# Sigmoid attention feeding a SiLU layer: a weight load in smaller pieces, another order of products in the output sets, and other stores at the end

## The chip, the cores and the metric

The kernel runs on one core of a Trainium2 chip. The metric is the time of one execution in microseconds (us) on the device; lower is better. TensorE (PE in the profile, PEld for its weight loads) multiplies matrices into PSUM, VectorE (DVE) and ScalarE (ACT) work on tiles, GpSimd (POOL) here issues all loads but the first, and SyncE (SP) issues the stores and the transposing DMAs.

## What is computed

Inputs are float32: q, k, v of shape (8, 12, 448, 64) and the weights w_in (768, 2048) and w_out (2048, 768).

```python
scores = (q @ k.transpose(0, 1, 3, 2)) / sqrt(64) - log(448)
attn = sigmoid(scores) @ v                      # (8, 12, 448, 64)
x = attn.transpose(0, 2, 1, 3).reshape(3584, 768)
h = x @ w_in
out = (h * sigmoid(h)) @ w_out                  # (3584, 768)
```

## The kernel before, in words

**Attention.** The work is cut into 24 groups g (a batch b and four of its heads). A group has seven chunks of keys. `scores` (L165) makes the 128x2x448 score tile of a chunk (64 keys, four heads) with four matmuls of 64 rows (L174), and ScalarE turns it into float16 with a sigmoid (L181). `values` (L191) multiplies the seven tiles by v (28 matmuls, L205) and scales the result into `xT`, the transposed input of the layer (L217, L221). The first six groups' q and k are transposed by TensorE (`pe_transpose`, L135), the rest by transposing DMAs.

**The layer.** The batches are taken in four pairs m. For the first pair `h_unit` (L234) makes one 128-column piece fc of h for one batch: six matmuls with w_in's columns fc*128 to fc*128+127 (L240), a sigmoid on ScalarE (L252) and a product on VectorE (L253). Pieces 0 to 7 need the first half of w_in's columns, pieces 8 to 15 the second half. After piece 8 and later ones of batch 0, VectorE also makes sums of w_in's blocks (`w_in_sums`, L272), the first of which reads all of the second half. For the later pairs `h_pair` (L300) uses a seven-product scheme in place of eight (in the manner of Strassen and Winograd). Its result lies in `gTr`.

**The output sets.** `out_set` (L442) multiplies two blocks of 128 rows by w_out with seven products of eight matmuls each (L463), also in the seven-product scheme. VectorE makes the sums S of the rows' blocks (`sg`, L478, L479, L484, L493), ScalarE copies the first product to `m1` (L481), and `plus` (L472) adds a product from PSUM to a block of the output tile `osb` (an eviction, L473). The output tiles are c11 and c12 (the two column halves of the first 128 rows) and c21 and c22 (of the second). `store` (L453) sends each tile in two halves of 64 rows (L455). There are 14 sets: three for each pair of batches, and one more after every second pair. The four that come first after a pair's h have a `tail`: their sums are made by then. The other ten make their own sums, at their start. In these, before the change, the order of the products is a1, a1 high, sg[2], sg[1], a2 high, sg[0], sg[3], with eight evictions. The very last set (`last`) computes c21 late and the last product in two halves of 192 columns.

**Order.** TensorE's order is written out by hand. `stretch` (L608) takes steps from the generator `all_moe` (L582) until its count of estimated nanoseconds is due, and between stretches `attend` (L746) puts in scores and values. Each `yield` is one matmul. The order on every engine is fixed when the program is built.

**Loads.** Loads go through POOL's queue, in program order, and convert to float16 on the way. `load` (L79) brings one group of q, k or v (224 KB as float16). `load_w_in(step, steps)` (L103) brings a range of w_in's columns with two DMAs, one for each half of its rows: at L642 and L644 a quarter of the columns each (384 KB a DMA), at L651 half of the columns (768 KB a DMA). `load_w_out` (L112) brings 768 KB. The calls stand in `after_transpose` (L640) and `after_values` (L648). Four buffers hold q and k, three hold v.

Of the kernel before, what the change touches and what calls it, by code (L numbers as in the profile page):

```python
# [17 lines left out]
def kernel(  # L18
# [9 lines left out]
    nc = tc.nc  # L28

    B, H, S, D = q.shape  # L30
    NT, DMODEL = out.shape
    DFF = moe_w_in.shape[1]
# [8 lines left out]
    NO2 = DMODEL // 2  # L41
    NQB = NQ * B
    NHC = NFC // 2
# [22 lines left out]
    def new_flat(name, g):  # L66
        flat[name, g] = (p3 if name == "v" else p4).tile(
            [P, 2, NCH, D], F16, tag=f"{name}f", name=f"{name}f"
        )

    def rows_in(name, g):
        b, iq = divmod(g, NQ)
        return (
            source[name][b]
            .rearrange("(j h) s d -> j h s d", j=2)[:, 2 * iq : 2 * iq + 2]
            .rearrange("j h (p c) d -> (h p) j (c d)", c=NCH)
        )

    def load(names, g, c0=0, c1=NCH):  # L79
        for name in names:  # L80
            if (name, g) not in flat:
                new_flat(name, g)
            nc.gpsimd.dma_start(  # L83
                flat[name, g][:, :, c0:c1].rearrange("p j c d -> p j (c d)"),
                rows_in(name, g)[:, :, c0 * D : c1 * D],
            )
# [13 lines left out]
    w_in_of = w_in_sb.rearrange("p (q h) f -> p h q f", h=2)  # L100
    w_out_sb = cpool.tile([P, NFC, DMODEL], F16, tag="w_out_sb", name="w_out_sb")

    def load_w_in(step, steps=1):  # L103
        cols = slice(step * DFF // 4, (step + steps) * DFF // 4)
        for j in range(2):
            rows = slice(j * DMODEL // 2, (j + 1) * DMODEL // 2)
            nc.gpsimd.dma_start(
                w_in_sb[j * D : (j + 1) * D, :, cols],
                moe_w_in[rows, cols].rearrange("(cc d) f -> d cc f", d=D),
            )  # L110

    def load_w_out(part):  # L112
        fcs = slice(part * NFC // 4, (part + 1) * NFC // 4)
        nc.gpsimd.dma_start(
            w_out_sb[:, fcs],
            moe_w_out[part * DFF // 4 : (part + 1) * DFF // 4].rearrange("(fc p) e -> p fc e", p=P),
        )
# [182 lines left out]
    def h_pair(m, tail):  # L300
# [112 lines left out]
    wq = [  # L413
        [w_out_sb[:, r * NHC : (r + 1) * NHC, c * NO2 : (c + 1) * NO2] for c in range(2)]
        for r in range(2)
    ]
    tw = {}
# [18 lines left out]
    def block(g):  # L436
        return gTr[:, :, g * P : (g + 1) * P]

    def row_blocks(m, g):
        return [rows_of[2 * m + u // NCH, u % NCH] for u in (2 * g, 2 * g + 1)]  # L440

    def out_set(a1, rows1, a2, rows2, scale, tail=(), last=False, halves=False):  # L442
        nonlocal hold
        lo, hi = slice(0, NHC), slice(NHC, NFC)
        osb = [p3.tile([P, DMODEL], F32, tag="osb", name="osb") for _ in range(2)]
        c11, c12 = (osb[0][:, nh * NO2 : (nh + 1) * NO2] for nh in range(2))
        c21, c22 = (osb[1][:, nh * NO2 : (nh + 1) * NO2] for nh in range(2))
        m1 = p3.tile([P, S], F32, tag="m1", name="m1")[:, :NO2]
        between, *sg = tail or [None]
        for i in range(len(sg) + 1, 4):  # L450
            sg.append(cpool.tile([P, NHC, P], F16, tag=f"S{i}", name=f"S{i}"))

        def store(rows, o, cols, engines):  # L453
            for at, (row, eng) in enumerate(zip(rows, engines)):
                eng.dma_start(row[:, cols], o[at * HP : (at + 1) * HP, cols])  # L455

        left, right, whole = slice(0, NO2), slice(NO2, DMODEL), slice(0, DMODEL)

        def product(a, w, between=None):
            po = ps_1.tile([P, 512], F32, tag="ps1", name="po")  # L460
            n = w.shape[2]
            for fc in range(NHC):
                nc.tensor.matmul(  # L463
                    po[:, :n], a[:, fc, :], w[:, fc, :], start=(fc == 0), stop=(fc == NHC - 1)
                )
                if fc < NHC - 1:
                    yield 163
                if between and fc == NHC // 2 - 1:
                    yield from between()
            return po[:, :n]  # L470

        def plus(o, po, x, sign=1.0):  # L472
            nc.vector.scalar_tensor_tensor(  # L473
                out=o, in0=po, scalar=sign * scale, in1=x, op0=ALU.mult, op1=ALU.add
            )

        if not tail:
            nc.vector.tensor_sub(sg[2], a1[:, lo], a2[:, lo])  # L478
            nc.vector.tensor_add(sg[0], a2[:, lo], a2[:, hi])  # L479
        po = yield from product(a1[:, lo], wq[0][0], between)  # L480
        nc.scalar.activation(m1, po, AF.Copy, scale=scale)  # L481
        sg.append(cpool.tile([P, NHC, P], F16, tag="S4", name="S4"))
        if not tail:
            nc.vector.tensor_sub(sg[1], sg[0], a1[:, lo])  # L484
        hold = False
        yield 163
        if tail:
            po = yield from product(sg[2], tw[3])
            plus(c22, po, m1)
            yield 163  # L490
        po = yield from product(a1[:, hi], wq[1][0])
        plus(c11, po, m1)
        nc.vector.tensor_sub(sg[3], a1[:, hi], sg[1])  # L493
        if last or halves:
            store(rows1, osb[0], left, (nc.sync, nc.sync))
        yield 163
        if not tail:
            po = yield from product(sg[2], tw[3])
            plus(c22, po, m1)
            yield 163  # L500
        po = yield from product(sg[1], tw[2])
        both = c21 if last else c22
        plus(both, po, c22)
        plus(c12, po, m1)
        yield 163

        def minus():
            po = yield from product(a2[:, hi], tw[4])
            plus(c21, po, both, -1.0)
            if not last:  # L510
                yield 163

        if not last:
            yield from minus()
        po = yield from product(sg[0], tw[1])
        plus(c22, po, both)
        plus(c12, po, c12)
        if last:
            yield 163
            yield from minus()  # L520
        store(rows2, osb[1], whole, (nc.sync, nc.scalar if last else nc.sync))
        yield 163
        for c0 in (0, NO2 // 2) if last else (0,):
            c1 = NO2 // 2 + c0 if last else NO2
            po = yield from product(sg[3], wq[1][1][:, :, c0:c1])
            plus(c12[:, c0:c1], po, c12[:, c0:c1])
            if last:
                store(rows1, osb[0], slice(NO2 + c0, NO2 + c1), (nc.sync, nc.scalar))
        if not last:
            store(rows1, osb[0], right if halves else whole, (nc.sync, nc.sync))  # L530
        yield 163

# [23 lines left out]
            if b * NFC + fc in rows_at:  # L556
                rows_of_quad(*rows_at[b * NFC + fc], act_copy)

    HALVES = 0

    def moe_set(m, g, tail=()):
        scale = ISX if m == 0 else 1.0
        step = out_set(
            block(g),
            row_blocks(m, g),
            block(g + 1),
            row_blocks(m, g + 1),
            scale,
            tail,
            halves=(m == B // 2 - 1 and g >= HALVES),  # L570
        )
        for i, ns in enumerate(step):
            if m % 2 == 0 and g == 2 and i % 8 == 4 and i < 32:
                fcs = slice(i // 8 * 4, i // 8 * 4 + 4)
                nc.vector.tensor_scalar_mul(kept[:, fcs], block(NCH - 1)[:, fcs], scale)
            if m == 0 and g == 2 and i in (36, 44, 52):
                next(in_sums)
            if m == 0 and g == 0 and i in (2, 8, 14, 20):
                next(sums)
            yield ns  # L580
# [59 lines left out]
    def after_transpose(g):  # L640
        if g == 0:
            load_w_in(0)  # L642
            load("kq", 4)
            load_w_in(1)  # L644
        elif g == 1:
            load("kq", 5)

    def after_values(g):  # L648
        if g == 0:
            load("v", 3)  # L650
            load_w_in(2, 2)  # L651
        elif g == 1:
            load("v", 4)
            load_w_out(0)
            load_w_out(2)
        elif g == 2:
            load("v", 5)
            load("kq", 6)
            load_w_out(1)
            load("kq", 7)  # L660
            load_w_out(3)
        elif 4 < g < NQB - 3:
            load("v", g + 3)
# [34 lines left out]
    def rounds(g, end):  # L698
        values(g, end)
        if end == NCH:  # L700
            after_values(g)
# [77 lines left out]
    n = 2 * NT_B  # L779
    for m in range(1, B // 2):  # L780
        stop = min(2 * (m + 1) * NT_B + 4, len(units))
        bursts = bursts_to(n, stop)
        n = stop
# [51 lines left out]
```

## Time and profile before

| | us |
|---|---|
| three runs | 364.54, 363.94, 367.28 |
| their median | 364.54 |
| the profiled execution | 367.21 |
| its span, from the first instruction's start to the last one's end | 365.1 |
| PE busy in it | 355.9 |
| DVE, ACT, POOL busy | 265.0, 249.7, 61.8 |

The profile is of one execution, the one of 367.21 us; 2.1 us of it lie outside the span. Lines are named L and a number. A row of the timeline gives the start, the busy time of a run of equal instructions and, in brackets, how long the engine had been idle before and what ended that. A landing is the moment when a DMA's completion is signalled. "POOL ... <- DMA x" in the list of waits means that POOL waited for the landing of x before it could issue.

### The profile page before, as it was taken

How to read it: one execution, taken by the hardware profiler on the slowest of the kernel's cores; microseconds unless marked ns; L12 is line 12 of the kernel's file. 1: busy time of each engine (PE TensorE's matmuls, PEld its weight loads, DVE VectorE, ACT ScalarE, POOL GpSimd, SP SyncE). 2: the span in 40 equal slices, each digit the busy share in tenths (PEclk: the TensorE clock that was granted, in tenths of full speed). 3: DMA queues.
4: the chain of work that ended last, by engine and by line, in shares of the span. 5: the costliest groups of instructions: out<-in, count | busy, mean ns of one | idle time of the engine just before them, and what ended most of it. 6: DMA issues, size and time to landing. Idle time of an engine off the chain costs nothing.

```text
span 365.1 us, 7677 instructions
## 1 busy us (share of the span) xinstructions
PE 355.9 (97%) x3029; PEld 182.9 (50%) x3029; DVE 265.0 (73%) x498; ACT 249.7 (68%) x363; POOL 61.8 (17%) x103
## 2 busy tenths in 40 slices
PE   8999799999999999999999999999999999999995
PEld 4544345444454555555445455555445455556663
DVE  3647479887879678787677667786777677778773
ACT  5998587697778767678777767758888766660000
POOL 8543210412505001100222201200100000000000
PEclk9999899999999999999999999999999999999999
DMA  8999999999899838405999752731965020003333
GB/s 136 196 205 210 208 206 170 135 195 139 139 202 175 147 95 114 59 0 96 172 165 216 148 113 50 105 49 24 154 95 133 19 69 0 3 0 87 88 87 85
DMA packets 63106, 42.78 MB, mean 117 GB/s; under 512 B 36064, under 2 KB 59232, under 8 KB 63072
## 3 DMA queue, kind: packets, MB, share of 16 engines
q0 software_dynamic: 24096, 22.58, 41.3%
q1 hardware_dynamic: 38592, 19.21, 26.9%
q10 hardware_dynamic: 384, 0.52, 0.4%
q8 instruction: 23, 0.38, 0.4%
q14 instruction: 11, 0.09, 0.1%
HBM read 45.61 MB, written 11.01 MB: 155 GB/s over the span
## 4 chain that ended last, share of the span: by engine, by line
PE 89%; DMA 9%; DVE 1%; issue 0%
PE po L463 36%; PE hy L316 11%; PE psc L174 10%; PE ph L240 8%; PE hz L316 7%; PE hx L316 7%; PE pav L205 7%; DMA w_in_sb<-in_moe_w_in_dram 5%; DMA kf<-in_k_dram 3%; DMA qs<-in_q_dram 1%; DVE qT L150 1%; PE ptrq L143 0%; PE pw L130 0%; PE ptrk L143 0%; DVE qf L633 0%
## 5 line engine op out<-in xcount | busy, mean ns | idle before, releaser
L181 ACT ACTIVATE attnT<-psc 128x896 f16<-128x896 f32 x168 | 144.9, 922 | 32.5 <-PE psc L174 29.9
L463 PEld LDWEIGHTS <-S 128*128 128x128 f16 x456 | 42.2, 98 | 35.5 <-issue 10.4
L174 PE MATMUL psc<-qT,kT 64*64 64x448 f16 x672 | 52.2, 361 | 1.0 <-DVE qT L150 0.7
L473 DVE SCALAR_TENSOR_TENSOR osb<-po,osb 128x384 f32<-128x384 f32 (+1 forms) x71 | 37.8, 549 | 15.9 <-PE po L463 15.0
L221 DVE TENSOR_SCALAR xT<-pav 128x448 f16<-128x448 f32 x44 | 25.6, 620 | 26.0 <-PE pav L205 26.0
L327 ACT ACTIVATE gTr<-u 128x448 f16<-128x448 f32 x48 | 27.6, 575 | 23.2 <-DVE u L340 19.1
L240 PE MATMUL ph<-xT,w_in_sb 128*128 128x448 f16 x192 | 40.5, 361 | 2.7 <-DMA w_in_sb<-in_moe_w_in_dram 2.6
L463 PE MATMUL po<-w_out_sb,S 128*128 128x384 f16 (+1 forms) x232 | 41.5, 321 | 0.0
L463 PE MATMUL po<-T,S 128*128 128x384 f16 x224 | 41.3, 327 | 0.0
L316 PEld LDWEIGHTS <-w_in_sb 128*128 128x128 f16 x288 | 28.2, 98 | 26.1
L463 PEld LDWEIGHTS <-gTr 128*128 128x128 f16 x304 | 28.3, 98 | 23.2 <-issue 5.8
L205 PE MATMUL pav<-attnT,vf 64*64 64x448 f16 x672 | 37.5, 349 | 0.0
L463 PE MATMUL po<-w_out_sb,gTr 128*128 128x384 f16 x192 | 35.7, 327 | 0.0
L316 PE MATMUL hy<-xs,w_in_sb 128*128 128x448 f16 x144 | 35.1, 353 | 0.0
L316 PE MATMUL hx<-xT,w_in_sb 128*128 128x448 f16 x144 | 34.6, 353 | 0.0
L316 PEld LDWEIGHTS <-W 128*128 128x128 f16 x216 | 21.1, 98 | 19.6
L174 PEld LDWEIGHTS <-kT 64*64 64x64 f16 x672 | 16.2, 104 | 28.8 <-issue 24.2
L83 POOL DMA_DIRECT2D vf<-in_v_dram x24 | 17.2, 718 | 71.6 <-PE psc L174 70.0
L240 PEld LDWEIGHTS <-w_in_sb 128*128 128x128 f16 x192 | 17.7, 99 | 23.0 <-issue 8.9
L473 DVE SCALAR_TENSOR_TENSOR osb<-po,m 128x384 f32<-128x384 f32 x42 | 23.0, 553 | 6.4 <-PE psc L174 1.7
L253 DVE TENSOR_TENSOR gTr<-ph,tsig 128x448 f16<-128x448 f32 x32 | 19.8, 623 | 9.1 <-ACT tsig L252 8.9
L205 PEld LDWEIGHTS <-vf 64*64 64x64 f16 x672 | 20.1, 107 | 11.5 <-issue 1.1
(76 smaller groups left out, 414.4 us busy)
## 6 DMA issues: line engine op xcount, KB each, us to landing
out_dram<-osb SPq DMA_DIRECT2D x47, 192.0 KB, 3.2
vf<-in_v_dram POOLq DMA_DIRECT2D x24, 224.0 KB, 7.8
kf<-in_k_dram POOLq DMA_DIRECT2D x23, 224.0 KB, 5.8
qf<-in_q_dram POOLq DMA_DIRECT2D x23, 224.0 KB, 6.8
w_out_sb<-in_moe_w_out_dram POOLq DMA_DIRECT2D x4, 768.0 KB, 18.4
w_in_sb<-in_moe_w_in_dram POOLq DMA_DIRECT2D x4, 384.0 KB, 11.4
w_in_sb<-in_moe_w_in_dram POOLq DMA_DIRECT2D x2, 768.0 KB, 15.1
out_dram<-osb SPq DMA_DIRECT2D x14, 96.0 KB, 2.2
```

Of the source, the lines that this page charges most:

```text
L83: nc.gpsimd.dma_start(flat[name, g][:, :, c0:c1].rearrange("p j c d -> p j (c d)"), rows_in(name, g)[:, :, c0 * D : c1 * D],)
L150: (copy[0] if copy else nc.vector.tensor_copy)(dst[:, c0 * P : c1 * P], ptr[:, : (c1 - c0) * P])
L174: nc.tensor.matmul(psc[own, j, :S], qkT["k", g][rows, ch, own], qkT["q", g][rows, :, own], start=True, stop=True,)
L181: nc.scalar.activation(attnT[g, ch], psc[:, :, :S], AF.Sigmoid, bias=NEG_LOG_S, scale=QKSCALE)
L205: nc.tensor.matmul(pav[half][j * D : (j + 1) * D, :S], flat["v", g][own, j, ch, :], at[own, j, :], start=(ch == 0), stop=(ch == NCH - 1),)
L221: nc.vector.tensor_scalar_mul(xT[b][:, half * NQ + iq, :], pav[half][:, :S], SX)
L240: nc.tensor.matmul(ph[:, :S], w_in_of[:, cc // NQ, cc % NQ, fc * P : (fc + 1) * P], xT[b][:, cc, :], start=(at == 0), stop=(at == NCC - 1),)
L253: nc.vector.tensor_mul(gTr[:, fc, (b % 2) * S : (b % 2) * S + S], ph[:, :S], tsig)
L316: nc.tensor.matmul(ps, a[:, c, i * P : (i + 1) * P], bs(c), start=(first and c == 0), stop=(c == HCC - 1), skip_group_check=True,)
L327: nc.scalar.activation(gTr[:, side * NHC + i, odd * S : (odd + 1) * S], src, AF.Silu, scale=ISX)
L463: nc.tensor.matmul(po[:, :n], a[:, fc, :], w[:, fc, :], start=(fc == 0), stop=(fc == NHC - 1))
L473: nc.vector.scalar_tensor_tensor(out=o, in0=po, scalar=sign * scale, in1=x, op0=ALU.mult, op1=ALU.add)
```

## The change

Three parts. First, the second half of w_in is loaded as two quarters (four DMAs of 384 KB) in place of one half (two of 768 KB), and among the loads before it group 4's q is moved behind w_in's second quarter. Second, in the ten sets without a tail, sg[1] is multiplied before sg[2], and c22 is started from c12, which already holds m1 plus sg[1]'s product; one eviction falls away, and sg[0] and sg[1] are now made at the set's start and sg[2] after the first product's copy. The four sets with a tail keep their products and evictions. Third, the very last set follows the same order as the others, computes c21 before sg[0]'s product, stores c21 and c22 as two column halves on the queues of SP and ACT, and makes and stores the last product's 384 columns in one piece.

```diff
-    def load_w_in(step, steps=1):
-        cols = slice(step * DFF // 4, (step + steps) * DFF // 4)
+    def load_w_in(step):
+        cols = slice(step * DFF // 4, (step + 1) * DFF // 4)
...
         if not tail:
-            nc.vector.tensor_sub(sg[2], a1[:, lo], a2[:, lo])
             nc.vector.tensor_add(sg[0], a2[:, lo], a2[:, hi])
+            nc.vector.tensor_sub(sg[1], sg[0], a1[:, lo])
         po = yield from product(a1[:, lo], wq[0][0], between)
         nc.scalar.activation(m1, po, AF.Copy, scale=scale)
+        if not tail:
+            nc.vector.tensor_sub(sg[2], a1[:, lo], a2[:, lo])
         sg.append(cpool.tile([P, NHC, P], F16, tag="S4", name="S4"))
-        if not tail:
-            nc.vector.tensor_sub(sg[1], sg[0], a1[:, lo])
...
+        po = yield from product(sg[1], tw[2])
+        if tail:
+            plus(c22, po, c22)
+        plus(c12, po, m1)
+        yield 163
         if not tail:
             po = yield from product(sg[2], tw[3])
-            plus(c22, po, m1)
+            plus(c22, po, c12)
             yield 163
-        po = yield from product(sg[1], tw[2])
-        both = c21 if last else c22
-        plus(both, po, c22)
-        plus(c12, po, m1)
+        po = yield from product(a2[:, hi], tw[4])
+        plus(c21, po, c22, -1.0)
+        if last:
+            store(rows2, osb[1], left, (nc.sync, nc.scalar))
         yield 163
-
-        def minus():
-            po = yield from product(a2[:, hi], tw[4])
-            plus(c21, po, both, -1.0)
-            if not last:
-                yield 163
-
-        if not last:
-            yield from minus()
         po = yield from product(sg[0], tw[1])
-        plus(c22, po, both)
+        plus(c22, po, c22)
         plus(c12, po, c12)
         if last:
-            yield 163
-            yield from minus()
-        store(rows2, osb[1], whole, (nc.sync, nc.scalar if last else nc.sync))
+            store(rows2, osb[1], right, (nc.sync, nc.scalar))
+        else:
+            store(rows2, osb[1], whole, (nc.sync, nc.sync))
         yield 163
-        for c0 in (0, NO2 // 2) if last else (0,):
-            c1 = NO2 // 2 + c0 if last else NO2
-            po = yield from product(sg[3], wq[1][1][:, :, c0:c1])
-            plus(c12[:, c0:c1], po, c12[:, c0:c1])
-            if last:
-                store(rows1, osb[0], slice(NO2 + c0, NO2 + c1), (nc.sync, nc.scalar))
-        if not last:
+        po = yield from product(sg[3], wq[1][1])
+        plus(c12, po, c12)
+        if last:
+            store(rows1, osb[0], right, (nc.sync, nc.scalar))
+        else:
             store(rows1, osb[0], right if halves else whole, (nc.sync, nc.sync))
         yield 163
...
             load_w_in(0)
-            load("kq", 4)
+            load("k", 4)
             load_w_in(1)
+            load("q", 4)
...
             load("v", 3)
-            load_w_in(2, 2)
+            load_w_in(2)
+            load_w_in(3)
```

The name HALVES, which was 0 and chose nothing, is dropped; `product` always takes 384 columns.

More of the change, by code (lines that the diff above doesn't have):

```diff
@@ L460, in product @@
             po = ps_1.tile([P, 512], F32, tag="ps1", name="po")
-            n = w.shape[2]
             for fc in range(NHC):
                 nc.tensor.matmul(
-                    po[:, :n], a[:, fc, :], w[:, fc, :], start=(fc == 0), stop=(fc == NHC - 1)
+                    po[:, :NO2], a[:, fc, :], w[:, fc, :], start=(fc == 0), stop=(fc == NHC - 1)
                 )
@@ L469, in product @@
                     yield from between()
-            return po[:, :n]
+            return po[:, :NO2]
         def plus(o, po, x, sign=1.0):
@@ L557, in moe_h @@
                 rows_of_quad(*rows_at[b * NFC + fc], act_copy)
-    HALVES = 0
     def moe_set(m, g, tail=()):
@@ L569, in moe_set @@
             tail,
-            halves=(m == B // 2 - 1 and g >= HALVES),
+            halves=(m == B // 2 - 1),
         )
```

## The prediction

> **What bounds the kernel now.** I read the page first, then TensorE's list of waits, then the timeline and the chain around its only long wait, then POOL's loads one by one, and last the end.
>
> ```profile
> PE 355.9 (97%) x3029; PEld 182.9 (50%) x3029; DVE 265.0 (73%) x498; ACT 249.7 (68%) x363; POOL 61.8 (17%) x103
> ```
> ```profile
> PE ph L240 <- DMA w_in_sb<-in_moe_w_in_dram: 2.6, 1, 2.6
> ...
> PE psc L174 <- DVE qT L150: 0.7, 2, 0.4
> ```
>
> TensorE is the bound. DVE has 100 us idle, so work taken from DVE pays only where TensorE waits for DVE, and the list has no such wait after 13 us. One wait of substance is left: h waits for w_in.
>
> ```profile
> 38.19 0.74 PE L240 MATMUL ph<-xT,w_in_sb 128*128 128x448 f16 x3
> ...
> 39.69 0.62 DVE L253 TENSOR_TENSOR gTr<-ph,tsig 128x448 f16<-128x448 f32 x1 [0.43 <-ACT tsig L252]
> ...
> 41.52 0.92 PE L240 MATMUL ph<-xT,w_in_sb 128*128 128x448 f16 x4 [2.59 <-DMA w_in_sb<-in_moe_w_in_dram]
> ```
>
> I counted the L240 matmuls: 48 stand before 41.52, so the waiting one begins piece 8, the first that reads w_in's second half. What the wait does to the clock is in the stretches (the column after POOL's is the granted clock) and in the chain:
>
> ```profile
> 42.00:43.00 1.00, 1.00 (x15) 0.28 (x14) 0.00 (x0) 0.20 (x1) 1.00 (x2) 0.90 1.13 204
> 43.00:44.00 1.00, 1.00 (x15) 0.72 (x15) 0.45 (x1) 1.00 (x2) 0.06 (x1) 0.50 1.19 215
> ...
> 47.00:48.00 1.00, 1.00 (x12) 0.41 (x5) 0.74 (x2) 1.00 (x2) 0.00 (x0) 1.00 1.22 203
> ```
> ```profile
> 9.00 0.51 PE ptrk L143 x14
> ...
> 42.94 0.89 PE ptrq L143 x14
> 43.83 3.00 PE ph L240 x9
> ...
> 47.33 1.81 PE ph L240 x9
> ```
>
> Right behind the wait the clock is half for 3.4 us, and 14 transposes and 9 matmuls take 0.89 and 3.00 us where their like take 0.51 and 1.81.
>
> The loads behind it, by POOL's timeline:
>
> ```profile
> 23.31 0.67 POOL L107 DMA_DIRECT2D w_in_sb<-in_moe_w_in_dram  x1 [0.87 <-DMA w_in_sb<-in_moe_w_in_dram]
> 24.83 0.66 POOL L107 DMA_DIRECT2D w_in_sb<-in_moe_w_in_dram  x1 [0.85 <-DMA kf<-in_k_dram]
> ...
> 30.75 0.70 POOL L83 DMA_DIRECT2D vf<-in_v_dram  x1 [0.40 <-issue]
> ```
>
> Asked load by load, the trace gives times to landing, which I add to the issues. v3 (issued at 21.74) lands at 33.14, the two 768 KB loads at 36.91 and 41.33, v4 at 41.81, v5 (the 30.75) at 50.45. Landings keep the order of issue, 10 to 20 us behind it, and each issue waits for the eighth load before it: it is a full queue, in which a landing is set by the bytes ahead. Neighbours in it land 1.15 us apart for 224 KB of q, k or v, and 1.56, 1.82, 1.76 and 1.73 apart (mean 1.72) for w_in's 384 KB.
>
> **The change part by part.** The sum is against the profiled execution, 367.21 us, which is 2.67 over the median of 364.54; what that means comes below.
>
> *w_in in quarters.* Four loads at 1.72 behind v3 land at 34.9, 36.6, 38.3 and 40.0; at the nearest row on the slow side (768 KB in 3.77 to 4.42, so 1.9 to 2.2 for half) the second lands at 36.9 to 37.6. Piece 8 needs the first two. TensorE asks for it at 38.76 (38.19 and three matmuls at 0.19), so the wait goes: 41.52-38.76 = 2.76. The half clock behind it goes with it: 0.38+1.19 = 1.57. Less what is late next: 1.35 us into piece 8 come transposes, then at 40.11, that take the PSUM buffer of piece 7, which DVE frees at 40.31 (39.69+0.62): 0.25 with the signal. Front: 2.76+1.57-0.25 = 4.08. Then DVE's first sum over the second half, at 45.85 before and some 42 then, needs the fourth quarter (40.0 to 41.3). Piece 12 asks at 47.1. Group 5's values, at 55.63 before, come at 51.55 and need v5, which lands at 49.8 to 50.5. All are covered, by 1 us at the least; without the cover, each microsecond of lateness costs one.
>
> *Two more issues, and q4 behind w_in's second quarter.* The issues cost POOL 2 x 0.66 us, inside its own waits; the queue holds over 10 us of work meanwhile. The second quarter lands 1.15 earlier, at 28.2 (29.32 before; piece 4 asks at about 29.95, so nothing is paid either way). q4 lands about 3.5 later, 29.3 for 25.83; its transposes run at 31.03. The bounds: no gain, or a wait if it were 1.7 later still. k5, q5 and v3 have the same bytes ahead and stay. I take 0.
>
> *Seven evictions.* Ten at 0.55 fall away, 5.5 us of DVE, worth 0 under the list of waits. The moved sums could cost: sg[1] now serves the third product and sg[2] the fourth. In the barest stretch, where no attention stretches TensorE's side, the rows are:
>
> ```profile
> 342.94 0.68 DVE L478 TENSOR_TENSOR S<-gTr 128x1024 f16<-128x1024 f16 x1
> 343.53 0.69 DVE L479 TENSOR_TENSOR S<-gTr 128x1024 f16<-128x1024 f16 x1
> ...
> 344.25 0.69 DVE L484 TENSOR_TENSOR S<-S,gTr 128x1024 f16<-128x1024 f16 x1
> 344.70 1.40 PEld L463 LDWEIGHTS <-S 128*128 128x128 f16 x9
> ```
>
> sg[0] at 342.94 and sg[1] 0.72 behind it are done at 344.35; the third product loads its weights at 344.70. The margin falls from 1.08 to 0.35. I went through all ten set starts in this way: three have 0.35, the others 0.9 or more. sg[2], done at 344.95, is needed at 346.0. Cost 0; below, nothing; above, 0.3 in three sets, 0.9. Behind the new dependence of c22 on c12 nothing waits but DVE itself, which runs in order.
>
> *The end.* Matmuls end as before (16 of 192 columns at a step of 0.083 against 8 at 0.163). The rows:
>
> ```profile
> 359.95 2.27 ACTq L455 DMA_DIRECT2D out_dram<-osb  x3
> 360.68 0.36 DVE L473 SCALAR_TENSOR_TENSOR osb<-po,osb 128x192 f32<-128x192 f32 x1 [0.30 <-PE po L463]
> ```
> ```profile
> out_dram<-osb SPq DMA_DIRECT2D x14, 96.0 KB, 2.2
> ...
> out_dram<-osb ACTq DMA_DIRECT2D x2, 48.0 KB, 2.9
> ```
>
> Before, the last eviction ends at 361.04, SP issues at 361.15, ACT only at 361.50 behind its two earlier issues, and the last landing is at 364.15 (2.64 later), the span's end 0.98 behind that. After, the last eviction (0.56) ends at 361.22, both queues are free, and issue at 361.28. c21's halves went 2.6 us earlier, c22's at 359.95. 96 KB with nothing beside it took 2.07; a 192 KB pair took 3.38 on its slower queue. So the landing is between 363.35 and 364.66, a gain of 0.8 or a loss of 0.5; nearest are the 96 KB rows, with something for the other queue: 2.4, so 363.7, a gain of 0.45. The last set issues eight stores before and after.
>
> Sum: 367.21-4.08-0.45 = 362.68.
>
> *Two rules of the Trainium skill beside these rows.* "TensorE: Matmul & The Clock Gate", section "HAM oscillation", says that idle gaps of more than some 3.4 us bring the half clock; here it follows a gap of 2.59. By that rule the dip is not the wait's doing, would stay, and the sum would be 364.25; it is rival 3. "DMA: Bandwidth & Descriptors", section "Anatomy of one DMA", gives each load about 2.0 us of fixed cost beside its bytes; taken as queue time that is an estimate of 3.8 us for a 384 KB load (786 KB of float32), against the 1.72 measured. By it the change loses; it is rival 4.
>
> **The rivals.**
> 1. The median run. After the first loads nothing but this wait depends on DMA timing, so most of the 2.67 by which the profiled run lies over the median is probably wait and dip that the faster runs lack. If they lack all of it, the result is 362.68. If they lack only the dip, it is 364.54-(2.76-0.25)-0.45 = 361.58. My forecast is the middle, 362.1. If they have both in full and the 2.67 lies outside: 364.54-4.53 = 360.0.
> 2. The faster runs hardly wait, the profile's wait is its own, and only the end gains: 364.1. For it: four times fall in two groups, near 364.2 and near 367.2, further apart than the dip. Against it: the load's landing is 2.6 us late, and the whole queue would have to be faster.
> 3. The dip has another cause and stays: 364.2. Against it: it is the only one in the run after the start, and stands right behind the only wait.
> 4. The other side: small loads take the queue longer. The place is v5 before group 5's values. The two big loads took 7.5 of the queue (41.81-33.14-1.15), so v5 lands at 50.45+4x-7.5 for x per load, and is needed at 51.55. From x = 2.2 it waits, from 3.3 (a wait of 4.5) the gain is gone, and at 4.42, the longest that any w_in load took in the trace, v5 lands at 60.6 and TensorE is 9.1 behind, so 362.7+9.1 = 371.8. Against it: four rows at 1.56 to 1.82 of just this shape.
>
> **The numbers.** Forecast (361.58 to 362.68, with the end's bounds 360.9 to 363.3) 0.58; the full gain on the median, 360.0, 0.14; rivals 2 and 3 together 0.20; rival 4 0.08. The range takes the forecast, the full gain's better-borne half and rivals 2 and 3: 359.8 to 364.4. What a measurement of this kernel can tell from no change is about 1%: faster means under 360.9, slower over 368.2. The full gain and 0.10 of the forecast's lower edge: 0.24 faster. Most of rival 4: 0.05 slower. Same: 0.71.
>
> **What would show it.** Right: no wait of ph L240 for w_in, a granted clock of 1.00 from 38 to 50 us, piece 8 begun by 39, landings of w_in about 1.7 apart, group 5's values near 51.5, seven evictions a set and no wait of PE for DVE's S at set starts, the last landing 2.4 us behind its issue. Wrong: a new wait of pav L205 for v5 or of a third product for sg[1], a dip elsewhere, or landings over 2.2 us apart.

## The result and the profile after

The changed kernel takes 363.04 us (median of 21 runs, 361.85 to 363.93), the kernel before 364.31 in the same series: a ratio of 0.9959, interval [0.9943, 0.9975]. In a later series it was 363.34 against 363.77, 0.9988 [0.9974, 1.0002]. By the medians it is 0.1 to 0.4% faster, within what I had called no change; the second interval reaches a ratio of 1. The forecast was 362.1, range 359.8 to 364.4.

TensorE's waits, from the profile of the changed kernel (engine and line, what it waited for, us in total, times, the longest):

```profile
PE pw L130 <- DVE warm L621: 1.1, 1, 1.1
PE ptrk L143 <- DMA kf<-in_k_dram: 1.0, 1, 1.0
PE po L462 <- DVE gTr L253: 0.8, 1, 0.8
PE psc L174 <- DVE qT L150: 0.7, 2, 0.4
```

The 2.6 us for w_in are gone. A wait of 1.0 in the first 7 us comes from a first load that landed later in this execution. The third line is new: the first output product waits for DVE. Before looking at it, the front, from the timeline and the stretches (the granted clock stands behind POOL's column):

```profile
38.48 1.50 PE L240 MATMUL ph<-xT,w_in_sb 128*128 128x448 f16 x7
39.91 0.57 PE L174 MATMUL psc<-qT,kT 64*64 64x448 f16 x8
40.41 0.58 PE L143 MATMUL ptrq<-ident,qf 128*64 128x128 f16 x14
```
```profile
38.00:40.00 2.00, 2.00 (x23) 0.81 (x19) 1.17 (x3) 1.95 (x3) 0.76 (x1) 1.00 1.21 207
40.00:42.00 2.00, 2.00 (x28) 1.07 (x29) 1.74 (x3) 1.66 (x3) 1.22 (x2) 1.00 1.18 216
42.00:44.00 2.00, 2.00 (x17) 0.75 (x15) 1.49 (x4) 1.86 (x5) 0.18 (x1) 1.00 1.15 206
```

The last three matmuls of piece 7 and the first four of piece 8 are now one run of seven, begun at 38.48, and the clock is 1.00 throughout. The four quarters landed at 34.31, 36.20, 38.16 and 40.03.

And the place of the new wait, in the changed kernel's timeline:

```profile
65.21 0.35 POOL L664 COPY seen<-qT 1x1 f16<-1x1 f16 x1 [15.35 <-DMA qT<-qr]
65.69 0.70 POOL L83 DMA_DIRECT2D vf<-in_v_dram  x1
66.38 0.71 POOL L83 DMA_DIRECT2D kf<-in_k_dram  x1
67.08 0.72 POOL L83 DMA_DIRECT2D qf<-in_q_dram  x1
...
73.85 0.62 DVE L158 COPY qr<-qf 128x896 f16<-128x896 f16 x1 [2.41 <-DMA qf<-in_q_dram]
...
75.45 1.15 DVE L253 TENSOR_TENSOR gTr<-ph,tsig 128x448 f16<-128x448 f32 x2
76.12 1.46 PE L462 MATMUL po<-w_out_sb,gTr 128*128 128x384 f16 x8 [0.79 <-DVE gTr L253]
```

DVE stands 2.41 us before its row copy (L158) of q of group 8, whose load, issued at 67.08, lands at 73.82. Behind the copy in DVE's queue are the last products of h (L253), and the first output product needs them. Before, the same rows read:

```profile
65.52 0.18 POOL L671 COPY seen<-qT 1x1 f16<-1x1 f16 x1 [14.96 <-DMA qT<-qr]
66.00 0.70 POOL L83 DMA_DIRECT2D vf<-in_v_dram  x1 [0.31 <-issue]
...
67.40 0.72 POOL L83 DMA_DIRECT2D qf<-in_q_dram  x1
...
75.31 0.61 DVE L158 COPY qr<-qf 128x896 f16<-128x896 f16 x1
```

There TensorE and DVE were 4 us later, and the copy at 75.31 came behind the landing at 74.24. POOL's little copy `seen`, which waits for group 6's transposed q, stands ahead of these loads, and it came at 65.21 for 65.52: the 4 us that the engines had won did not reach it. The rows of the transposing DMAs show where they were lost, first the changed kernel's, then those of before:

```profile
55.05 1.48 SPq L159 DMA_TRANSPOSE kT<-kr  x1
57.32 3.30 SPq L159 DMA_TRANSPOSE qT<-qr  x1
```
```profile
59.08 1.33 SPq L159 DMA_TRANSPOSE kT<-kr  x1
61.35 1.22 SPq L159 DMA_TRANSPOSE qT<-qr  x1
```

They were issued 4 us earlier and landed at 64.38 and 65.15 against 64.64 and 65.46. The queue of loads was busy until about 64 us in both kernels: the last load of w_out lands at 62.32 and 62.41, and behind it v of group 8 at 63.91 and 63.62. In all 14 profiles of this study group 6's transposed k lands 0.4 to 1.0 us behind that load of v, whether it was issued at 54.5 or at 59.1. That the busy queue holds the transposes back is inferred from this; no run takes the loads away. What was won on TensorE ran into the DMA queue's own end.

The gate is not the whole of it. Behind the gate, k of group 8 lands at 70.80 and q 3.03 later, at 73.82, where neighbours of this size in the full queue come some 1.1 apart. The other profile of the changed kernel has 3.88, the kernel before 1.72. No run here shows why.

The end, changed kernel:

```profile
355.58 3.10 ACTq L455 DMA_DIRECT2D out_dram<-osb  x3
356.29 1.02 DVE L472 SCALAR_TENSOR_TENSOR osb<-po,osb 128x384 f32<-128x384 f32 x2 [0.74 <-PE po L462]
357.59 0.56 DVE L472 SCALAR_TENSOR_TENSOR osb<-po,osb 128x384 f32<-128x384 f32 x1 [0.28 <-PE po L462]
```
```profile
out_dram<-osb SPq DMA_DIRECT2D x17, 96.0 KB, 2.2
...
out_dram<-osb ACTq DMA_DIRECT2D x3, 96.0 KB, 2.4
```

The last eviction ends at 358.15, both queues issue at 358.18, and the last landing is 2.38 later.

One table splits every profile by three marks of its timeline: TensorE's first scores, its first output product, its last matmul's end. The start of the first scores (6.2 to 7.2 us) is left out. The kernels that differ from these two are explained with the experiments.

| profile | first scores to first output product | to the last matmul's end | to the span's end |
|---|---|---|---|
| before | 72.79 | 281.44 | 4.49 |
| before, another execution | 70.18 | 281.44 | 4.49 |
| changed | 69.30 | 281.44 | 3.97 |
| changed, another execution | 70.01 | 281.43 | 3.99 |
| before, quarters alone | 70.33 | 281.44 | 4.51 |
| before, new order of the sets alone | 69.43 | 281.45 | 4.53 |
| before, new end alone | 69.85 | 281.44 | 3.98 |
| changed, group 8's k and q ahead of v | 68.36 | 281.42 | 3.95 |
| the same, another execution | 69.43 | 284.20 | 3.97 |
| the same with halves | 68.91 | 281.44 | 3.97 |
| changed, quarters in the other order | 70.16 | 281.44 | 3.96 |
| changed, eighths | 71.27 | 281.42 | 3.97 |
| before, w_in behind v of group 4 | 70.59 | 281.44 | 4.47 |
| before, q of group 4 alone | 70.02 | 281.74 | 4.49 |

All 14 sets and three pairs of batches lie in the middle column. It stays within 0.03 us but for two profiles: 0.30 more with q of group 4 alone, at the values near 118 us and for no reason that I know, and 2.78 more in one execution in which scores waited for transposed q (another of the same kernel has 281.42). The end gives 0.5. The rest of the difference is the front. Profiled executions of kernels with w_in in halves and without the half clock (before again, the new sets alone, the new end alone) have 69.43 to 70.18 there, and the changed kernel 69.30 and 70.01: at the front, these profiles show hardly any gain left.

### The profile page after: what moved, and what is told of

It reads as the page before. It is cut to its first block, busy times and chain, and to the rows that moved or that the text cites. A ratio compares the mean times of both kernels' runs of the same rounds, so it can differ in the third digit from the quotient of the medians.

```text
span 361.5 us, 7653 instructions
## 1 busy us (share of the span) xinstructions
PE 353.7 (98%) x3021; PEld 181.6 (50%) x3021; DVE 260.3 (72%) x487; ACT 249.7 (69%) x363; POOL 63.1 (17%) x105
## 4 chain that ended last, share of the span: by engine, by line
PE 87%; issue 5%; DMA 3%; ACT 3%; DVE 1%; POOL 1%; POOLq 0%
PE po L462 37%; PE hy L316 11%; PE psc L174 10%; PE hz L316 8%; PE hx L316 8%; PE pav L205 8%; PE ph L240 4%; ACT attnT L181 3%; DMA qf<-in_q_dram 2%; DMA kf<-in_k_dram 1%; PE ptrk L143 1%; DVE qT L150 1%; PE ptrq L143 0%; POOL vf L83 0%; PE pw L130 0%
## 5 line engine op out<-in xcount | busy, mean ns | idle before, releaser
L472 DVE SCALAR_TENSOR_TENSOR osb<-po,osb 128x384 f32<-128x384 f32 x70 | 37.6, 554 | 19.7 <-PE po L462 18.9
L462 PE MATMUL po<-w_out_sb,S 128*128 128x384 f16 x224 | 41.3, 327 | 0.0
L240 PE MATMUL ph<-xT,w_in_sb 128*128 128x448 f16 x192 | 39.2, 353 | 0.0
L253 DVE TENSOR_TENSOR gTr<-ph,tsig 128x448 f16<-128x448 f32 x32 | 19.7, 622 | 7.3 <-ACT tsig L252 7.0
L383 DVE TENSOR_TENSOR u<-hy,p 128x448 f32<-128x448 f32 x24 | 15.0, 625 | 13.8 <-PE hy L316 13.4
```

Of the source, the lines that this page charges most:

```text
L240: nc.tensor.matmul(ph[:, :S], w_in_of[:, cc // NQ, cc % NQ, fc * P : (fc + 1) * P], xT[b][:, cc, :], start=(at == 0), stop=(at == NCC - 1),)
L253: nc.vector.tensor_mul(gTr[:, fc, (b % 2) * S : (b % 2) * S + S], ph[:, :S], tsig)
L383: nc.vector.tensor_add(u3, y, p1)
L462: nc.tensor.matmul(po[:, :NO2], a[:, fc, :], w[:, fc, :], start=(fc == 0), stop=(fc == NHC - 1))
L472: nc.vector.scalar_tensor_tensor(out=o, in0=po, scalar=sign * scale, in1=x, op0=ALU.mult, op1=ALU.add)
```

## The experiments

My theory (A): the front has two limits in a row, the wait for w_in and, behind it, the late q of group 8; the change lifts the first and runs into the second, and the execution that I predicted from had an unusually long first wait. The rivals are named with each run.

**The kernel before again.** No edit.

> The kernel before, unchanged, to see whether its wait for w_in and the half clock behind it belong to every execution. Theory A (the usual execution has a shorter wait and no dip, the profiled one of 367.2 us had both): ratio 1.000 within 0.4%; most runs near 364 with a mean granted clock of 0.997 or more, a few near 366 to 368 with 0.993; if the new profile is one of the usual ones, TensorE waits 0.5 to 1.8 us for w_in before piece 8 and the clock stays 1.00 between 42 and 47 us. Theory B (every execution has the full wait of 2.6 us and the dip, and the spread lies outside): the new profile shows both again whatever its time, and the clock is 0.993 in all runs.

Ratio 0.9995 [0.9972, 1.0018]; clocks of 0.998 to 1.000 in all ten runs. Its timeline at piece 8:

```profile
38.51 0.74 PE L240 MATMUL ph<-xT,w_in_sb 128*128 128x448 f16 x3
40.38 0.92 PE L240 MATMUL ph<-xT,w_in_sb 128*128 128x448 f16 x4 [1.13 <-DMA w_in_sb<-in_moe_w_in_dram]
41.23 0.57 PE L174 MATMUL psc<-qT,kT 64*64 64x448 f16 x8
41.73 0.58 PE L143 MATMUL ptrq<-ident,qf 128*64 128x128 f16 x14
```

The load lands at 40.24, not 41.33; the wait is 1.13, and 14 transposes take 0.58, as in the changed kernel: full clock. Theory A holds: the front is 2.61 us shorter than in the first profile, which had the long wait and the dip. None of these ten runs is one of the longer kind that it expected; two of the 35 runs of the kernel before in the same series are (367.85 us with a mean clock of 0.993, 366.27 with 0.995).

**The quarters alone**, in the kernel before:

```diff
-            load_w_in(2, 2)
+            load_w_in(2)
+            load_w_in(3)
```

> The kernel before with one edit: w_in's second half in two quarters; q of group 4, the output sets and the end as before. Theory A (the gain is the wait for w_in, and part of it is given back where q of group 8 lands late): no wait of piece 8, group 5's values near 51.6 us, DVE waits 1.5 to 3 us for q of group 8 and the first output product 0.4 to 1.2 us for DVE; ratio 0.997 (0.9955 to 0.9985), most of the change's 0.9959. Theory B (the loads matter only in disturbed executions, the gain is the sets and the end): ratio 1.000.

363.87 against 364.33; 0.9978 [0.9954, 1.0001]. No wait of piece 8, but

```profile
74.73 0.62 DVE L158 COPY qr<-qf 128x896 f16<-128x896 f16 x1 [3.39 <-DMA qf<-in_q_dram]
...
76.33 1.15 DVE L253 TENSOR_TENSOR gTr<-ph,tsig 128x448 f16<-128x448 f32 x2
77.00 1.46 PE L463 MATMUL po<-w_out_sb,gTr 128*128 128x384 f16 x8 [1.70 <-DMA kf<-in_k_dram]
```

The last row names a load of k, but the product starts at 77.00 right behind the first of DVE's two products of h in the row above it (0.62 us each from 76.33), as it does in the changed kernel. The second limit takes 1.70, more than I had expected, and in this profile (a front of 70.33) all that an execution with a wait of 1.13 had to give. The rows show the mechanism of theory A, the wait gone and part of it given back, but the front of this execution gains nothing, as theory B has it, and the interval of the times reaches both: what the quarters alone are worth is not shown here.

**The sets alone**: the changed `out_set` for nine sets, the old one for the very last, in the kernel before.

```diff
-        step = out_set(
+        step = out_set_new(
...
-                yield from out_set(
+                yield from (out_set if m == B // 2 - 1 else out_set_new)(
```

> The kernel before with the new order of products and seven evictions in nine of the ten sets without a tail (the very last set, the loads and the stores as before). Theory A (DVE's work is hidden): DVE is busy some 5 us less, no product waits for a sum, ratio 1.000 within 0.2%. Theory B (part of the gain is that TensorE waits less for DVE, hidden in its busy time): ratio 0.998 or less.

DVE is busy 261.1 us in place of 264.6, less of a saving than the 5 that I expected; the middle column is 281.45. The ratio is 0.9977 [0.9955, 0.9999], which misses the 0.2% that I gave it by a hair and lies where theory B put it. But the columns of the table that the edit touches do not move, and TensorE waits there for nothing, which speaks against B. So I put these 0.2% down to the front, which the edit does not touch; that is not shown, and the times alone can't decide it.

**The end alone**: the mirror image, the changed `out_set` for the very last set.

```diff
-                yield from out_set(
+                yield from (out_set_new if m == B // 2 - 1 else out_set)(
```

> The kernel before with the new very last set alone (order, stores by halves on two queues, the last product in one piece). Theory A: the last landing comes 2.4 us behind its issue in place of 2.6 behind an issue that stood 0.35 us in the queue; 0.4 to 0.6 us less, ratio 0.9987 (0.998 to 0.9995). Theory B (what follows the last landing takes up the difference): ratio 1.000.

363.58 against 364.33, 0.998 [0.9957, 1.0002]; from the last matmul to the span's end 3.98 against 4.49. The rows give half a microsecond, as in the changed kernel; theory A. The medians differ by 0.75, with an interval that reaches 1.

**The changed kernel again**, no edit.

> The changed kernel, unchanged, beside the next kernel. Every theory: ratio 0.996 (0.994 to 0.998). The theory that q of group 8 is late in every execution, not in one profile alone: DVE waits 1 to 3.5 us before its row copy of q (L158) near 71 to 74 us, and the first output product 0.4 to 1.7 us.

363.34 against 363.77. Its timeline has the second limit once more, larger:

```profile
74.27 0.62 DVE L158 COPY qr<-qf 128x896 f16<-128x896 f16 x1 [3.19 <-DMA qf<-in_q_dram]
...
76.54 1.46 PE L462 MATMUL po<-w_out_sb,gTr 128*128 128x384 f16 x8 [1.49 <-DVE gTr L253]
```

**The second limit lifted**, in the changed kernel:

```diff
             if g == 6:
-                load("v", 6)
                 load("kq", 8)
+                load("v", 6)
                 load("v", 7)
```

> The changed kernel with k and q of group 8 loaded ahead of v of group 6 in place of behind it. Theory A (q of group 8 lands behind DVE's row copy, DVE stands, and the first output product waits for h's last pieces; this gives back 0.8 us or more of the front's gain): q of group 8 lands by 71.5 us, DVE's wait before the copy is under 0.5 us, the first output product waits for nothing, 0.6 to 1.0 us less than the changed kernel, ratio 0.994. Theory B (the wait there is harmless or moves on to v of group 6 or to another load): the same ratio as the changed kernel's, and a new wait of pav L205 for v.

362.09, against 363.34 of the changed kernel in the same series, and 0.9958 [0.9942, 0.9974] to before: 1.25 us from the order of three loads, where I had expected 0.6 to 1.0.

```profile
65.69 0.71 POOL L83 DMA_DIRECT2D qf<-in_q_dram  x1
...
70.78 0.61 DVE L158 COPY qr<-qf 128x896 f16<-128x896 f16 x1
...
74.67 1.46 PE L462 MATMUL po<-w_out_sb,gTr 128*128 128x384 f16 x8
```
```profile
PE pw L130 <- DVE warm L621: 1.1, 1, 1.1
PE psc L174 <- DVE qT L150: 0.7, 2, 0.4
```

q lands at 69.70, the copy follows k's at once, the product waits for nothing, and v of group 6 (71.73) is not missed. This is the fastest version of the study.

**That version again, and with halves.** First no edit; then w_in's second half as two 768 KB loads.

> The changed kernel with k and q of group 8 ahead of v of group 6, unchanged from the last call, beside the next kernel. Every theory: 362.0 to 362.6, ratio 0.995 (0.9935 to 0.9965); from TensorE's first scores to the first output product 68.2 to 68.6 us; no wait of TensorE for data after 13 us.

362.32 (twelve runs), 0.9959 [0.9935, 0.9983]. The profiled execution was its slowest, 366.55, with waits that I had not expected: 2.4 us of the scores for transposed q, 0.8 for a first load of k, and a start 0.9 us late; its front, 69.43, missed the 68.2 to 68.6 that I gave it. The first output product waits for nothing in it. The eleven others lie at 361.83 to 363.71.

```diff
-            load_w_in(2)
-            load_w_in(3)
+            load_w_in(2, 2)
```

> The same with w_in's second half as two 768 KB loads again, so that only the size of these loads differs. Theory A (two limits in a row: the wait for w_in, and behind it q of group 8; each hides part of the other's price): with the second limit gone the wait for w_in is paid in full, 0.9 to 1.6 us more than with quarters, no wait before the first output product, ratio 0.998 (0.9965 to 0.9995). Theory B (the quarters themselves bring nothing, the order of group 8's loads brings all): the same time as with quarters, ratio 0.995.

363.32 (twelve runs, 362.53 to 364.64), 1.0 us more than with quarters in the same series; 0.9976 [0.9956, 0.9995]. So by the medians the quarters are worth about 1 us once the second limit is away, and theory B falls. In its own profile the wait for w_in was only 0.23, and the front 0.55 longer than in the first profile with quarters (68.91 and 68.36), so the executions differ, and where each of them pays the 1 us is not shown.

**The quarters in the other order**, in the changed kernel, so that piece 8 needs all four loads:

```diff
-            load_w_in(2)
             load_w_in(3)
+            load_w_in(2)
```

> The changed kernel with the two second-half quarters in the other order, so that piece 8 needs all four loads, as with the halves. Theory A (what matters is how many bytes stand ahead of the columns that piece 8 reads): they land at 40.0, TensorE waits 1.0 to 1.6 us, no half clock, the given-back wait shrinks; ratio 0.997 to 0.999, near the usual execution before less the end's 0.5 us. Theory B (the loads' size matters, smaller ones being quicker on the queue): no wait, ratio 0.996.

363.81, 1.0007 [0.9984, 1.003], above the range of both theories, though the interval still reaches A's. TensorE waits 0.7 us at piece 8 (the fourth load lands at 39.51) and again 0.8 at the first output product. The wait is back with small loads, so what counts is the bytes ahead; my 1.0 to 1.6 was too long and the second limit did not shrink as I had thought.

**Eighths**, in the changed kernel: `load_w_in(step, 8)` for steps 4 to 7.

> The changed kernel with w_in's second half in eight loads of 192 KB in place of four of 384 KB. Theory A (in the full queue a landing is set by the bytes ahead): neighbours land 0.8 to 1.0 us apart, v of group 4 at 40.6 to 41.8 as before, ratio 0.996 to 0.999 like the changed kernel. Theory B (each load has a fixed price of some 2 us on the queue): landings 2.5 us or more apart, v of group 5 behind 57 us, a new wait of pav L205 of 4 us or more, ratio 1.01.

Neighbours land 0.65, then 0.98 to 1.05 us apart, v of group 4 at 42.04, a little behind the 41.8 that I gave it; 0.9987 [0.9968, 1.0007]. Two 192 KB loads take 2.0 us where one of 384 KB took 1.9: a load more costs 0.1 us in the full queue, not 2. Theory A. The second limit takes 2.06 us in this profile, the most of all, and 0.59 is a wait for w_in's first half, whose loads the edit does not touch; so this one profile says little on what eighths are worth.

**w_in behind v of group 4**, in the kernel before:

```diff
             load("v", 3)
-            load_w_in(2, 2)
         elif g == 1:
             load("v", 4)
+            load_w_in(2, 2)
```

> The kernel before with the 768 KB loads of w_in issued behind v of group 4, about 1.2 us later in the queue. Theory A (the half clock is the wait's doing, once the wait is some 2.5 us long): waits of 2.2 to 2.8 us, the dip in many of the runs (granted clock 0.993 to 0.995), and those runs 2.5 us or more above the usual 364. Theory B (the dip has a cause of its own and gaps under 3.4 us leave the clock alone): the same wait, no dip, runs near 365.3.

366.88 (four runs), 1.009 [1.0057, 1.0123]. The profiled one, 365.04:

```profile
40.93 0.92 PE L240 MATMUL ph<-xT,w_in_sb 128*128 128x448 f16 x4 [2.08 <-DMA w_in_sb<-in_moe_w_in_dram]
41.78 0.57 PE L174 MATMUL psc<-qT,kT 64*64 64x448 f16 x8
```
```profile
41.00:43.00 2.00, 2.00 (x28) 0.90 (x28) 0.26 (x1) 0.79 (x1) 0.70 (x1) 1.00 1.17 211
```

A wait of 2.08, and no dip. Two of the others, at 367.19 and 369.01, had mean clocks of 0.992 and 0.995; the fourth, 366.56, had 1.000. Only the first has a profile, so where the clock fell in the two is not shown; the profile before, with its dip, has a mean of 0.993. Neither theory fits all four: it looks as if a wait of this length brings the dip in some executions and not in others. In 33 executions of the changed kernel the mean clock was never under 0.997, but neither was it in the 24 of the kernel before in this last series, and one of the ten with the quarters in the other order, whose profile has a wait of 0.7, had 0.995.

**q of group 4 alone**, in the kernel before:

```diff
-            load("kq", 4)
+            load("k", 4)
             load_w_in(1)
+            load("q", 4)
```

> The kernel before with q of group 4 behind w_in's second quarter, nothing else. Every theory that I hold: the second quarter lands about 1.1 us earlier, q of group 4 at 28.5 to 29.5, neither is waited for, ratio 1.000 within 0.2%. If a wait of the transposes of q of group 4 appears, the 1.7 us of margin that I gave it were wrong.

1.0001 [0.9976, 1.0025]. The second quarter lands at 27.80, q of group 4 at 28.97, neither is waited for. Piece 8 waits 1.51 us for w_in's second half, as in the kernel before.

## Why the prediction was right, and where it was not

The time lay in the range and the class was the one forecast, 0.9 us above the number. That alone confirms little: the range held the full gain as well as hardly any, and the forecast was the middle between two guesses at what the usual execution waits. The rows confirm the mechanism, but for one step.

- *The wait and the dip go.* Right. The quarters landed within 0.6 us of 34.9, 36.6, 38.3 and 40.0, the later ones with some luck: they came 1.91 apart in place of 1.72, but v of group 3 ahead of them landed at 32.38 in place of 33.14. From the first scores to the start of h's last matmul the two profiles differ by 4.44 us (72.60 and 68.16) where I had 4.08. The 0.25 for a PSUM buffer did not show: the transposes began at 40.41, before DVE had ended its product of piece 7 (39.98 and 0.62).
- *"All are covered, by 1 us at the least."* This is the step that failed. Group 5's values came at 51.60 for v5 at 49.76, as worked out, but I followed the loads only to the last of w_out. Behind it POOL's queue had a gate, `seen`, and behind that q of group 8 and a DVE copy ahead of h's last pieces. The first output product began 1.14 us after the start of h's last matmul in place of 0.19: 0.95 given back. In the other execution of the changed kernel it was 1.84, so 1.65 given back.
- *The profiled execution and the median.* Right in kind: the usual execution lacks the dip and over half of the wait (1.13 for 2.59). So what it has to gain at the front is about 1.1 us and not 4, and by the profiles the second limit takes most of it. How the usual gain divides is not settled: the medians differ by 1.27 us in the first series and by 0.43 in the later one, and of that the rows give 0.5 to the end.
- *q behind w_in's second quarter: 0.* Right; ratio 1.0001.
- *Seven evictions: 0.* Right by the middle column. sg[1] is done 0.36 us ahead of the third product's weights, where I had 0.35:

```profile
340.58 0.69 DVE L478 TENSOR_TENSOR S<-S,gTr 128x1024 f16<-128x1024 f16 x1
341.19 0.68 DVE L482 TENSOR_TENSOR S<-gTr 128x1024 f16<-128x1024 f16 x1
341.63 2.54 PEld L462 LDWEIGHTS <-S 128*128 128x128 f16 x16
```

- *The end: 0.45.* 0.52, with a landing of 2.38 for the 2.4 taken.
- *The sum.* 362.68 was meant for an execution that now took 363.34: +0.95 given back, -0.36 at the front, -0.07 at the end, +0.41 by a later first score, -0.27 outside the span, in all +0.66.
- *Rivals.* 1 held. 2 (the usual run hardly waits) was nearer the truth than the 0.20 that it shared: the wait there is 1.13, and the end's 0.5 is a large part of the usual gain. 3 fell, as far as one dip can show it: the dip stood behind the longest wait, and no other profile has one between the first scores and the last matmul. By the Trainium skill ("TensorE: Matmul & The Clock Gate", section "HAM oscillation") it takes a gap of more than some 3.4 us; this case's profile shows it behind one of 2.59, and none behind 2.08 and 1.13. 4 fell: 0.1 us for a load more, where the Trainium skill's fixed 2.0 us ("DMA: Bandwidth & Descriptors", section "Anatomy of one DMA") would have shown as spacing if each load took it in the queue.

What stays open is why the landing of w_in differs by 1 us between executions of one program, and why the same wait brings the dip only sometimes. On the first, v of group 3 ahead of it explains 0.36 (33.14 and 32.78); the rest is the second 768 KB load, 4.42 behind the first in place of 3.70, while v of group 4 behind it is only 0.48 later. On the second, the profiles have more to read. TensorE had stopped at 38.93 (38.19 and 0.74) and gone on at 41.52 when the clock fell, at 42.8. At the end of the kernel TensorE also stands idle, and there the clock falls 3.0 us behind the last matmul in the profile before (360.64), 2.4 in that of the new sets alone (357.19), and in that of w_in behind v of group 4 not within 4.5 (358.48, full clock until the span's end at 363.0). So no fixed length of gap fits these traces.

## What to carry to other kernels

When a stall ahead of a saturated DMA queue is taken away, walk the queue to its end, through every instruction that gates a later issue, before calling the rest covered: here the engines came 4 us earlier to a load that could not. One profile tells the mechanism and not the price; where the profiled time lies well off the median, price the stall from a second execution. And the order of a few loads can be worth as much as their size: moving two ahead of one that is needed later gave 1.25 us, quarters in place of halves 1.0.

## What the runs showed of the hardware that was not expected

- A transposing DMA issued at 55.05, while loads were in the queue, took 9.3 us to land where the same one issued 4 us later took 5.6; both landed 0.5 to 1.0 us behind the last load ahead.
- The half clock came behind a gap of 2.59 us, for 3.4 us, and not behind one of 2.08. With TensorE idle at the end of the kernel it came 2.4 us after the last matmul in one profile and not within 4.5 in another.
- In the full queue a 192 KB load lands 1.0 us behind its neighbour, one of 384 KB 1.9, one of 768 KB 3.7 to 4.4.
